# The eight pieces of the shrink in a spectral mixer: two halves, one slot apart, on VectorE alone

## The chip, the cores and the metric

The kernel runs on one NeuronCore of one Trainium2 chip. The metric is the device time of one execution in microseconds (us). A profile of one execution stands beside the times; its span reaches from the first to the last instruction of the program.

## The reference

```python
X = np.fft.rfft(x, axis=1)                  # x: 8 batches x 3072 tokens x 256
Yr = Xr @ w_r - Xi @ w_i + b_r
Yi = Xr @ w_i + Xi @ w_r + b_i
Yr = np.sign(Yr) * np.maximum(np.abs(Yr) - lam, 0.0)      # lam = 0.01
Yi = np.sign(Yi) * np.maximum(np.abs(Yi) - lam, 0.0)
y = np.fft.irfft(Yr + 1j * Yi, n=3072, axis=1)
h = y @ w_in                                # 256 -> 2048
out = (np.maximum(h, 0) + np.log1p(np.exp(-np.abs(h)))) @ w_out     # softplus, 2048 -> 256
```

The step that the change touches is the one with `lam`, the soft threshold. The kernel calls it the shrink: `z - clip(z, -lam, lam)`.

## The kernel before

**The work.** The Fourier transforms are done as products with small matrices in several steps: `s1`, `s3` (forward, with a transposition through memory between them), `mix` (the product with the weights, the bias, the shrink), `s4` (inverse, first half), and `s5` (inverse, second half, which gives tokens). The two layers of the network behind them take most of TensorE's time. All products that need it are done with three matmuls on values split in a high and a low part (`mm3`): the high part is a rounded copy that ScalarE makes, the low part is the rest, which VectorE makes by a subtraction (`low`, L719, and `less`, L119).

**The loop.** The network runs over 192 keys (batch, pair of token blocks, pair of hidden blocks), and each key over four slots, 0 to 3. A slot is written out by hand: first the products of the first layer (`slot_products`), then one step of the transform of a later batch if there is one in this slot (`steps`: one of `s1_four`, `s3`, `mix`, `s4_pair`, `s5`), then small preparations (`fill`: loads, and `fold`, two VectorE operations on the next input), then what earlier slots have put off (`later`), and at last the products of the second layer (`slot_second`). Instructions go to each engine in just this order, and each engine takes them in order.

**The two banks.** The first layer of a key is done with the products of Strassen's kind, seven instead of eight. They are collected in two banks of PSUM, `psc` and `pse`. The three adds of a key that involve `pse` are VectorE's (`add`, L703): it reads `pse` in slots 0, 2 and 3. The matmul that next writes `pse` (slots 1, 3 and 0 of the next key) must come after that add has read it. Behind an add follow, for the same values, ScalarE's softplus (L709), its rounding to the high part (L713), and VectorE's low part (L719), which the second layer needs.

**The mix.** Batches 1 to 7 have 12 mixes each (84), made by `mix_sums`, each one step of one slot. Its 18 to 24 matmuls of 256 columns are followed on VectorE by two adds to `z` (L487, L490), the clipping to `cl` (L491), and the shrink itself: eight pieces (L499) of 32 partitions by 256 columns, since each piece also moves its rows to another place of the tile. The eight pieces are a loop over `e` (the half of the target's partitions), `c` and `g`. In batch 1 the four pieces with `e` = 1 were given to GpSimd, beside VectorE's four. Batch 0 has another mix and isn't touched. The tile `shrunk` is read by `s4_pair`, which takes two mixes at once and stands three (batch 1) or four slots behind the second of them.

The pieces before:

```python
        for e in range(2):
            for c in range(2):
                for g in range(2):
                    src = slice(g * 64 + e * 32, g * 64 + e * 32 + 32), slice(c * D, c * D + D)
                    dst = slice(e * 64 + c * 32, e * 64 + c * 32 + 32), slice(g * D, g * D + D)
                    (nc.gpsimd if b == 1 and e and POOL1 else v).tensor_tensor(out=t[dst], in0=z[src], in1=cl[src], op=ALU.subtract)
```

Of the kernel before, what the change touches and what calls it, by code (L numbers as in the profile page):

```python
# [14 lines left out]
ALU = mybir.AluOpType  # L15
# [13 lines left out]
A22, A11, A12, S1, S2, S3, S4 = range(7)  # L29
B11, B21, T2, T3, T1, B22, T4 = range(7)  # L30
LAM = 0.01
POOL1 = True


@with_exitstack
def tile_spectral_mixer_mlp(ctx, tc, x, w_r, w_i, bias, bias_0, w_in, w_out, f, f_hi, f_lo, g1, g3, g3_hi, g3_lo, hm, out):
# [12 lines left out]
    nc = tc.nc  # L49
# [42 lines left out]
    later = deque()  # L92

    stored = Counter()
# [4 lines left out]
    def store(dst, src, what):  # L99

        queue = nc.scalar if early and what[0] == "d" and stored[what] >= 8 else nc.sync

        def start():
            queue.dma_start(dst, src)
            stored[what] += 1

        later.append(start)
# [140 lines left out]
    def mm3(ps, wh, wl, xh, xl, start, stop, more=False):  # L248
        nc.tensor.matmul(ps, wh, xh, start=start, stop=False, skip_group_check=more)  # L249
        nc.tensor.matmul(ps, wh, xl, start=False, stop=False, skip_group_check=more)  # L250
        nc.tensor.matmul(ps, wl, xh, start=False, stop=stop, skip_group_check=more)  # L251


    def psf():

        if early:
            early.append(None)
            if len(early) % 3:
                return ps_o.tile([P, 512], F32, tag="o", name="psf")
        return ps_f.tile([P, 512], F32, tag="f", name="psf")  # L260
# [182 lines left out]
    def mix(b, gp):  # L443
        assert stored["l", b, gp] == 2
        (mix_direct if b == 0 else mix_sums)(b, gp, *l_t.pop((b, gp)))
# [24 lines left out]
    def mix_sums(b, gp, lh, ll, real):  # L470

        v = nc.vector
        p1, ps = psf(), psf()

        def product(o, what, c, start, stop):
            for k in range(2):
                h, l = [t[:, k, what] if what < 3 else t[:, k] for t in ((lh, ll) if what < 3 else real)]
                mm3(o, h, l, wmh[:, k, c], wml[:, k, c], start and k == 0, stop and k == 1)

        product(p1[:, :D], 2, 0, True, True)  # L480
        product(ps[:, :D], 1, 1, True, True)
        product(ps[:, D:], 0, 2, True, not real)
        if real:
            product(ps[:, D:], 3, 0, False, True)
        z, cl = [sb.tile([P, 512], F32, tag=t, name=t, bufs=1) for t in ("z", "cl")]
        p3 = p1.rearrange("p (c n) -> p c n", c=2)[:, 0:1, :].to_broadcast([P, 2, D])
        v.tensor_tensor(out=z.rearrange("p (c n) -> p c n", c=2), in0=p3, in1=bias_sb, op=ALU.add)  # L487
        if gp == 0:
            v.tensor_tensor(out=z[0:1, D:], in0=p1[0:1, :D], in1=bias_sb[0:1, 0], op=ALU.add)
        v.tensor_tensor(out=z, in0=ps, in1=z, op=ALU.add)  # L490
        v.tensor_scalar(out=cl, in0=z, scalar1=-LAM, scalar2=LAM, op0=ALU.max, op1=ALU.min)  # L491

        t = sb.tile([P, 512], F32, tag=("sh", "sl")[gp % 2], name="shrunk", bufs=1)
        for e in range(2):
            for c in range(2):
                for g in range(2):
                    src = slice(g * 64 + e * 32, g * 64 + e * 32 + 32), slice(c * D, c * D + D)
                    dst = slice(e * 64 + c * 32, e * 64 + c * 32 + 32), slice(g * D, g * D + D)
                    (nc.gpsimd if b == 1 and e and POOL1 else v).tensor_tensor(out=t[dst], in0=z[src], in1=cl[src], op=ALU.subtract)  # L499
        s_t[b, gp] = t  # L500

    def s4(b, gp):
# [18 lines left out]
    def s4_pair(b, pp):  # L521

        if pp == 0:
            d_dr[b] = dram.tile([N1, N2, D], F32, tag="d", name="d_dr")
        banks = psf(), psf()
        both = [s_t.pop((b, 2 * pp + j)) for j in range(2)]
        for j in range(2):
            for kind, c in ((1, slice(0, 512)),) if pp or j else ((0, slice(0, D)), (1, slice(D, 512))):
                for e in range(2):
                    rows, cols = slice(64 * e, 64 * e + 64), slice(64 * j, 64 * j + 64)  # L530
                    nc.tensor.matmul(banks[e][cols, c], g3_half[rows, kind], both[j][rows, c], start=True, stop=True)
        for e, ps in enumerate(banks):
            d = sb.tile([P, 512], F32, tag="d", name="d")
            nc.scalar.copy(d, ps)
            row = 16 * pp + 8 * e
            store(d_dr[b][row:row + 8].rearrange("(g q) n c -> (q n) g c", g=2), d.rearrange("p (g c) -> p g c", g=2), ("d", b))
# [259 lines left out]
    with tc.manual_schedule():  # L796
# [23 lines left out]
        def plan_mix(b, start, step):  # L820
            mixed = done = start
            for gp in range(NP):
                t = product(max(start + step * gp, mixed), s3, b, gp)
                at(max(t - 4, 11), load_a, b, gp)
                mixed = done = product(max(t + (3 if gp else 4), done + 1), mix, b, gp)
                if gp % 2:
                    done = product(mixed + (3 if b == 1 else 4), s4_pair, b, gp // 2)
# [78 lines left out]
        for i in range(min([*fill, *steps]), nt * B + 3):  # L906
            due = len(later)
            if i >= 0:
                g, s = divmod(i, 4)
# [116 lines left out]
```

## Time and profile before

| | |
|---|---|
| median of 3 runs | 2708.27 us (2707.92 to 2711.35) |
| profiled execution, its own time | 2708.41 us |
| its span | 2706.3 us |
| TensorE (PE) busy | 2600.9 us, 96% |
| VectorE (DVE) busy | 1756.7 us, 65% |
| ScalarE (ACT) busy | 1634.7 us, 60% |
| GpSimd (POOL) busy | 201.3 us, 7% |

A row of the timeline says when an instruction began (us from the span's start), how long it took, its engine, line and operation, the tile it writes and those it reads, and in brackets how long its engine had stood idle before it and what it waited for. Matmuls overlap, so their starts tell more than their durations: two matmuls of 512 columns in a row start 0.23 us apart. Names of tiles are the program's: `pse` and `psc` are the two banks, `pso` the banks of the second layer, `psf` those of the transform.

### The profile page before, as it was taken

To read this page: it belongs to the slowest core of one execution; us is meant where nothing else is said; L and a number is where in the kernel's file an instruction comes from. 1 tells how busy PE (TensorE), PEld (TensorE's weight loads), DVE (VectorE), ACT (ScalarE), POOL (GpSimd) and SP (SyncE) were. 2 spreads that over 40 slices of the span, in tenths; PEclk is the share of its full clock that TensorE was granted. 3 is DMA by queue.
4 is the path that set the end of the run, shared out by engine and by line. 5 is a ranking of instruction groups with operands and counts; after the bars stand their busy time and mean duration, and the time that the engine had idled before them with its cause. 6 is when DMAs were issued, how large, how long until landed. Compare 5 with 4: busy or idle time off the path is not lost.

```text
span 2706.3 us, 36636 instructions
## 1 busy us (share of the span) xinstructions
PE 2600.9 (96%) x13252; PEld 2089.2 (77%) x13252; DVE 1756.7 (65%) x3016; ACT 1634.7 (60%) x2940; POOL 201.3 (7%) x245
## 2 busy tenths in 40 slices
PE   8899999999999999999999999999999999999999
PEld 5677778777787777877778777787777787788887
DVE  4888766676566765667756677566774666644554
ACT  4666556556665556665566556665566555666665
POOL 2322210000000000000000000000000000000000
PEclk9999999999999999999999999999999999999999
DMA  7875555655655555464565555556545455455543
GB/s 230 257 227 185 173 166 176 189 170 162 189 166 174 168 166 188 161 190 152 171 194 172 166 175 157 188 171 178 180 152 178 156 160 180 138 159 176 179 153 111
DMA packets 186944, 472.37 MB, mean 175 GB/s; under 512 B 22236, under 2 KB 88700, under 8 KB 186764
## 3 DMA queue, kind: packets, MB, share of 16 engines
q1 hardware_dynamic: 182780, 466.07, 55.0%
q0 software_dynamic: 2624, 2.32, 0.4%
q8 instruction: 105, 1.72, 0.3%
q10 hardware_dynamic: 1360, 1.64, 0.2%
q14 instruction: 75, 0.61, 0.1%
HBM read 382.89 MB, written 82.71 MB: 172 GB/s over the span
## 4 chain that ended last, share of the span: by engine, by line
PE 74%; DVE 19%; issue 2%; DMA 2%; ACT 2%; POOL 1%; SPq 0%; DVEq 0%; ACTq 0%; POOLq 0%
PE pso L249 10%; PE pso L251 10%; PE pso L250 10%; DVE shrunk L499 8%; PE psc L249 5%; PE psc L251 5%; PE pse L249 5%; PE psc L250 5%; PE pse L251 4%; PE pse L250 4%; PE psf L570 4%; PE psf L251 2%; PE psf L249 2%; PE psf L250 2%; DVE t L703 2%
## 5 line engine op out<-in xcount | busy, mean ns | idle before, releaser
L719 DVE TENSOR_TENSOR gl<-t,gh 128x512 fp32r<-128x512 f32 x768 | 537.6, 700 | 322.0 <-ACT gh L713 319.8
L698 ACT COPY t<-psc 128x512 f32<-128x512 f32 x576 | 337.6, 586 | 541.5 <-PE psc L251 540.6
L703 DVE TENSOR_TENSOR t<-pse,t 128x512 f32<-128x512 f32 x576 | 396.1, 688 | 404.5 <-ACT t L698 289.5
L249 PE MATMUL pso<-gh,w 128*128 128x512 f32 x1536 | 627.6, 409 | 0.0
L251 PE MATMUL pso<-gh,w 128*128 128x512 f32 x1536 | 601.4, 392 | 0.0
L250 PE MATMUL pso<-gl,w 128*128 128x512 f32 x1536 | 601.0, 391 | 0.0
L713 ACT CAST gh<-t 128x512 fp32r<-128x512 f32 x768 | 476.9, 621 | 61.9 <-PE pso L251 37.9
L709 ACT ACTIVATE t<-t 128x512 f32<-128x512 f32 x576 | 365.2, 634 | 149.5 <-DVE t L703 149.5
L249 PEld LDWEIGHTS pso<-gh,w 128*128 128x128 f32 x1536 | 290.3, 189 | 121.4 <-issue 72.7
L251 PEld LDWEIGHTS pso<-gh,w 128*128 128x128 f32 x1536 | 289.3, 188 | 63.6
L250 PEld LDWEIGHTS pso<-gl,w 128*128 128x128 f32 x1536 | 290.4, 189 | 48.7
L249 PE MATMUL psc<-y_sb,w 128*128 128x512 f32 x768 | 301.9, 393 | 7.3 <-ACT t L709 3.6
L249 PE MATMUL pse<-y_sb,w 128*128 128x512 f32 x576 | 235.1, 408 | 74.1 <-DVE t L703 73.4
L251 PE MATMUL psc<-y_sb,w 128*128 128x512 f32 x768 | 299.9, 391 | 0.0
L250 PE MATMUL psc<-y_sb,w 128*128 128x512 f32 x768 | 299.2, 390 | 0.0
L499 DVE TENSOR_TENSOR shrunk<-z,cl 32x256 f32<-32x256 f32 x624 | 275.9, 442 | 10.1
L609 POOL TENSOR_TENSOR y_sb<-raw,y_sb 128x512 fp32r<-128x512 f32 x69 | 99.1, 1437 | 2083.8 <-ACT y_sb L606 2083.6
L250 PE MATMUL pse<-y_sb,w 128*128 128x512 f32 x576 | 225.1, 391 | 0.2 <-DVE y_sb L625 0.2
L251 PE MATMUL pse<-y_sb,w 128*128 128x512 f32 x576 | 225.1, 391 | 0.0
L249 PEld LDWEIGHTS pse<-y_sb,w 128*128 128x128 f32 x576 | 108.1, 188 | 131.8 <-DVE t L703 110.3
L249 PEld LDWEIGHTS psc<-y_sb,w 128*128 128x128 f32 x768 | 144.5, 188 | 41.9 <-ACT t L709 6.2
L251 PEld LDWEIGHTS psc<-y_sb,w 128*128 128x128 f32 x768 | 144.4, 188 | 31.6
(167 smaller groups left out, 3225.5 us busy)
## 6 DMA issues: line engine op xcount, KB each, us to landing
w<-w_dr SPq DMA_DIRECT2D x190, 896.0 KB
w<-w_dr SPq DMA_DIRECT2D x185, 512.0 KB
out_y<-ot SPq DMA_DIRECT2D x96, 256.0 KB
dp<-d_dr SPq DMA_DIRECT2D x57, 384.0 KB
ap<-a_dr SPq DMA_DIRECT2D x168, 128.0 KB
d_dr<-d SPq DMA_DIRECT2D x84, 256.0 KB
x<-in_x SPq DMA_DIRECT2D x104, 192.0 KB
a_dr<-a SPq DMA_DIRECT2D x102, 192.0 KB
```

What stands on the lines that cost most here:

```text
L249: nc.tensor.matmul(ps, wh, xh, start=start, stop=False, skip_group_check=more)
L250: nc.tensor.matmul(ps, wh, xl, start=False, stop=False, skip_group_check=more)
L251: nc.tensor.matmul(ps, wl, xh, start=False, stop=stop, skip_group_check=more)
L499: (nc.gpsimd if b == 1 and e and POOL1 else v).tensor_tensor(out=t[dst], in0=z[src], in1=cl[src], op=ALU.subtract)
L570: nc.tensor.matmul(ps[:, t - blk * BLK:t - blk * BLK + n], d_sb[b, blk // 2, n2 // 4][0][:, n2 % 4, k * P:(k + 1) * P], d_sb[b, blk // 2, ...
L609: eng.tensor_tensor(out=lo, in0=raw[j], in1=hi.bitcast(F32), op=ALU.subtract)
L698: nc.scalar.copy(t, banks[bank])
L703: nc.vector.tensor_tensor(out=t, in0=banks[bank], in1=t, op=ALU.add)
L709: nc.scalar.activation(t, banks[bank] if bank else t, AF.Softplus)
L713: nc.scalar.copy(gh, ct[key, what])
L719: nc.vector.tensor_tensor(out=gl, in0=ct.pop((key, what)), in1=gh.bitcast(F32), op=ALU.subtract)
```

## The change

The four pieces with `e` = 0 stay where they were. The four with `e` = 1 are put on the list `later`, so they are issued in the next slot, behind that slot's own products, step and preparations. All are VectorE's now, in batch 1 too. A counter asserts that both halves have been issued before `s4_pair` reads the tile.

```diff
-POOL1 = True
@@ mix_sums
         t = sb.tile([P, 512], F32, tag=("sh", "sl")[gp % 2], name="shrunk", bufs=1)
-        for e in range(2):
+
+        def lay(e):
             for c in range(2):
                 for g in range(2):
                     src = slice(g * 64 + e * 32, g * 64 + e * 32 + 32), slice(c * D, c * D + D)
                     dst = slice(e * 64 + c * 32, e * 64 + c * 32 + 32), slice(g * D, g * D + D)
-                    (nc.gpsimd if b == 1 and e and POOL1 else v).tensor_tensor(out=t[dst], in0=z[src], in1=cl[src], op=ALU.subtract)
+                    v.tensor_tensor(out=t[dst], in0=z[src], in1=cl[src], op=ALU.subtract)
+            stored["s", b, gp] += 1
+
+        lay(0)
+        later.append(lambda: lay(1))
         s_t[b, gp] = t
@@ s4_pair
         both = [s_t.pop((b, 2 * pp + j)) for j in range(2)]
+        assert stored["s", b, 2 * pp + 1] == 2
```

VectorE's order behind a mix in slot 2 with no step in the next slot (batch 3, eighth mix), before. `gl` is a low part, `t<-pse` the add that reads the bank, numbers tell tiles apart:

```order
L491 TENSOR_SCALAR cl_8650<-z_8649 128x512
L499 TENSOR_TENSOR shrunk_8654<-z_8649,cl_8650 32x256 x8
L719 TENSOR_TENSOR gl_8684<-t_8626,gh_8678 128x512
L703 TENSOR_TENSOR t_8613<-pse_8606,t_8613 128x512
L719 TENSOR_TENSOR gl_8708<-t_8680,gh_8682 128x512
L703 TENSOR_TENSOR t_8703<-pse_8699,t_8703 128x512
```

The same place in the changed program, whose lines from the pieces on are five lower:

```order
L490 TENSOR_SCALAR cl_8650<-z_8649 128x512
L499 TENSOR_TENSOR shrunk_8654<-z_8649,cl_8650 32x256 x4
L724 TENSOR_TENSOR gl_8680<-t_8626,gh_8674 128x512
L708 TENSOR_TENSOR t_8613<-pse_8606,t_8613 128x512
L499 TENSOR_TENSOR shrunk_8654<-z_8649,cl_8650 32x256 x4
L724 TENSOR_TENSOR gl_8708<-t_8676,gh_8678 128x512
L708 TENSOR_TENSOR t_8703<-pse_8699,t_8703 128x512
```

The second half has moved behind the first low part and add, and stands ahead of the second ones.

VectorE's order behind a mix in slot 2 with an `s3` in the next slot (batch 3, seventh mix), before. `l<-psf` and `sum` are the two operations of `s3` on VectorE, `ot` is a store's copy:

```order
L499 TENSOR_TENSOR shrunk_8507<-z_8502,cl_8503 32x256 x8
L740 COPY ot_8528<-pso_7443 128x512
L719 TENSOR_TENSOR gl_8543<-t_8479,gh_8537 128x512
L703 TENSOR_TENSOR t_8450<-pse_8443,t_8450 128x512
L119 TENSOR_TENSOR l_8551<-psf_8546,l_8551 128x2x256
L421 TENSOR_TENSOR sum_8552<-psf_8546,sum_8552 128x256
L719 TENSOR_TENSOR gl_8582<-t_8539,gh_8541 128x512
L703 TENSOR_TENSOR t_8577<-pse_8573,t_8577 128x512
```

And in the changed program:

```order
L499 TENSOR_TENSOR shrunk_8507<-z_8502,cl_8503 32x256 x4
L745 COPY ot_8524<-pso_7443 128x512
L724 TENSOR_TENSOR gl_8539<-t_8479,gh_8533 128x512
L708 TENSOR_TENSOR t_8450<-pse_8443,t_8450 128x512
L118 TENSOR_TENSOR l_8547<-psf_8542,l_8547 128x2x256
L420 TENSOR_TENSOR sum_8548<-psf_8542,sum_8548 128x256
L499 TENSOR_TENSOR shrunk_8507<-z_8502,cl_8503 32x256 x4
L724 TENSOR_TENSOR gl_8582<-t_8535,gh_8537 128x512
L708 TENSOR_TENSOR t_8577<-pse_8573,t_8577 128x512
```

The second half has moved behind the add of the next slot and behind both operations of `s3`.

VectorE's order behind a mix in slot 1 with an `s3` in the next slot (batch 3, fifth mix), before:

```order
L499 TENSOR_TENSOR shrunk_8185<-z_8180,cl_8181 32x256 x8
L703 TENSOR_TENSOR t_8207<-pse_8149,t_8207 128x512
L119 TENSOR_TENSOR l_8215<-psf_8210,l_8215 128x2x256
L421 TENSOR_TENSOR sum_8216<-psf_8210,sum_8216 128x256
L719 TENSOR_TENSOR gl_8244<-t_8207,gh_8238 128x512
L703 TENSOR_TENSOR t_8156<-pse_8149,t_8156 128x512
```

And in the changed program:

```order
L499 TENSOR_TENSOR shrunk_8185<-z_8180,cl_8181 32x256 x4
L708 TENSOR_TENSOR t_8203<-pse_8149,t_8203 128x512
L118 TENSOR_TENSOR l_8211<-psf_8206,l_8211 128x2x256
L420 TENSOR_TENSOR sum_8212<-psf_8206,sum_8212 128x256
L499 TENSOR_TENSOR shrunk_8185<-z_8180,cl_8181 32x256 x4
L724 TENSOR_TENSOR gl_8244<-t_8203,gh_8238 128x512
L708 TENSOR_TENSOR t_8156<-pse_8149,t_8156 128x512
```

Here too the second half has moved behind the first add and the operations of `s3`, and stands ahead of the second add. The orders of TensorE and ScalarE are the same in both programs; GpSimd loses 48 pieces.

## Rows read from the trace of the kernel before

**Rows 1.** Page, part 1: busy us (share of the span) xinstructions.

```profile
PE 2600.9 (96%) x13252; PEld 2089.2 (77%) x13252; DVE 1756.7 (65%) x3016; ACT 1634.7 (60%) x2940; POOL 201.3 (7%) x245
```

**Rows 2.** Waits of TensorE, whole span: us in total, times, longest us.

```profile
PE pse L249 <- DVE t L703: 73.4, 73, 2.6
...
PE psc L249 <- ACT t L709: 3.6, 6, 0.6
```

**Rows 3.** Waits of TensorE in the mixes of batch 1, then of batch 3.

```profile
PE pse L249 <- DVE t L703: 5.4, 8, 1.4
...
PE pse L249 <- DVE t L703: 11.1, 10, 2.6
```

**Rows 4.** Groups of instructions by form, VectorE: xcount | busy us, mean ns | idle.

```profile
L499 DVE TENSOR_TENSOR shrunk<-z,cl 32x256 f32<-32x256 f32 x624 | 275.9, 442 | 10.1
```

**Rows 5.** Timeline behind the eighth mix of batch 3, ScalarE, VectorE and TensorE.

```profile
935.21 0.62 ACT L713 CAST gh<-t 128x512 fp32r<-128x512 f32 x1
...
936.54 3.42 DVE L499 TENSOR_TENSOR shrunk<-z,cl 32x256 f32<-32x256 f32 x8
...
939.72 0.39 PE L251 MATMUL psc<-y_sb,w 128*128 128x512 f32 x1
...
940.00 0.69 DVE L719 TENSOR_TENSOR gl<-t,gh 128x512 fp32r<-128x512 f32 x1
...
940.61 0.68 DVE L703 TENSOR_TENSOR t<-pse,t 128x512 f32<-128x512 f32 x1
...
941.35 0.50 PE L249 MATMUL pse<-y_sb,w 128*128 128x512 f32 x1 [1.24 <-DVE t L703]
...
941.68 0.39 PE L250 MATMUL pse<-y_sb,w 128*128 128x512 f32 x1
...
942.15 1.06 PE L365 MATMUL psf<-ap 128*128 128x128 f32 x8
...
944.41 0.39 PE L249 MATMUL psc<-y_sb,w 128*128 128x512 f32 x1
```

**Rows 6.** Timeline of TensorE behind the mix of batch 3 with a fold.

```profile
834.97 0.50 PE L249 MATMUL pse<-y_sb,w 128*128 128x512 f32 x1 [2.57 <-DVE t L703]
...
835.77 1.50 PE L365 MATMUL psf<-ap 128*128 128x128 f32 x8
...
839.62 0.41 PE L249 MATMUL psc<-y_sb,w 128*128 128x512 f32 x1
```

**Rows 7.** Stretch behind it: length, TensorE busy (x), granted clock, DMA share, GB/s.

```profile
836.90:839.60 2.70, 2.70 (x8) 0.50 1.04 233
```

**Rows 8.** Timeline behind the seventh mix of batch 3, VectorE and TensorE.

```profile
928.82 0.68 DVE L703 TENSOR_TENSOR t<-pse,t 128x512 f32<-128x512 f32 x1
...
930.28 0.39 PE L249 MATMUL pse<-y_sb,w 128*128 128x512 f32 x1
```

**Rows 9.** Timeline behind the fifth mix of batch 3, VectorE, ScalarE and TensorE.

```profile
888.06 3.43 DVE L499 TENSOR_TENSOR shrunk<-z,cl 32x256 f32<-32x256 f32 x8
...
889.91 0.59 ACT L380 CAST l<-psf 128x512 fp32r<-128x512 f32 x1
...
892.27 0.50 PE L249 MATMUL pse<-y_sb,w 128*128 128x512 f32 x1 [0.61 <-DVE t L703]
...
894.17 0.68 DVE L703 TENSOR_TENSOR t<-pse,t 128x512 f32<-128x512 f32 x1
...
895.13 0.40 PE L249 MATMUL pse<-y_sb,w 128*128 128x512 f32 x1
```

**Rows 10.** Timeline behind the tenth mix of batch 3, ScalarE and TensorE.

```profile
978.99 0.59 ACT L592 CAST y_sb<-psf 128x512 fp32r<-128x512 f32 x1 [0.70 <-PE psf L570]
...
983.98 0.50 PE L249 MATMUL psc<-y_sb,w 128*128 128x512 f32 x1 [0.60 <-ACT t L709]
```

**Rows 11.** Timeline behind the fourth mix of batch 1, VectorE.

```profile
251.92 3.04 DVE L499 TENSOR_TENSOR shrunk<-z,cl 32x256 f32<-32x256 f32 x4
...
254.99 1.12 DVE L719 TENSOR_TENSOR gl<-t,gh 128x512 fp32r<-128x512 f32 x1
```

## The prediction, made before the changed kernel ran

> **What bounds the kernel now.** I read the page's first part, then the waits of TensorE, then those waits in single batches, then the timeline around one wait of each kind. TensorE is busy 96% of the span [rows 1], so only time that it stands still can be won. The table of waits names one large cause: the first matmul into the bank pse waits for VectorE's add at L703, 73.4 us in 73 waits [rows 2]; everything else after the start is small (ScalarE's softplus into psc: 3.6 us in 6). One middle batch holds 11.1 us of it in 10 waits, batch 1 holds 5.4 in 8 [rows 3]. The waits stand behind the mixes of batches 1 to 7: pse is read by an add; that add stands on VectorE behind the shrink's eight pieces of the mix one slot earlier; and TensorE may not write pse before the add has read it. VectorE's pieces are 275.9 us in all [rows 4], and VectorE as a whole is far from full (65%, [rows 1]): its order hurts, not its load.
>
> **What one wait costs.** Take the eighth mix of batch 3 [rows 5]. The pieces run from 936.54 for 3.42 us (0.43 each), then the low part at L719 (940.00), then the add (940.61). TensorE's matmul into pse starts at 941.35, 0.74 after the add's start. The matmul before it was issued at 939.72 and matmuls follow each other by 0.23, so pse was due at 939.95: 1.40 lost. The next one comes 0.33 behind instead of 0.23, another 0.10. So a wait that reads 1.24 in its row costs 1.50.
>
> **The change, part by part.** No arithmetic goes away. 4 of 8 pieces (4 x 0.43 = 1.72 us) leave their slot and stand at the end of the next slot's VectorE work; in batch 1, 12 x 4 pieces come over from GpSimd. TensorE, ScalarE and the queues keep their order, and the pair product that reads the shrunk tile comes at least two slots after the second half, so nobody waits for that half itself. What counts is which add stands behind which half. There are five kinds of mix.
>
> (a) *Mix in slot 2 or 3 of a key, no s3 in the next slot:* 25 of 84 (four each in batches 2 to 6, five in batch 7), all with the wait of rows 5. After: the first half ends at 936.54 + 1.72 = 938.26. The low part can go at once (its input was written by 935.83, [rows 5]), the add 0.61 later at 938.9, TensorE at 939.64, before 939.95. No wait is left, with 0.3 to spare. The second half then runs to 941.3, and the next low part and add follow at 941.3 and 941.9, which frees the bank at 942.7; the next matmul into pse then comes about 943.6 (without the s3 step in that stretch, 942.6). So the second half fits, in the tightest case by nothing. 25 x 1.50 = **37.5 us**.
>
> (b) *The same with a fold behind the pieces:* 5 mixes (batches 2 to 6). [...] From the s3 product to the second psc behind it takes 839.62 - 835.77 = 3.85 [rows 6], where the same work in rows 5 takes 944.41 - 942.15 = 2.26: the clock costs 1.6. After: the add is 1.72 sooner, the wait reads about 0.85. Waits up to 1.24 leave the clock at full speed (the matmuls behind 941.35 in rows 5 are 0.23 apart soon after), so I take the clock's part as won too: 5 x (1.72 + 1.59) = **16.5 us**.
>
> (c) *Slot 2, with s3 behind it:* 12 mixes in batches 2 to 7. The first add is free, as in (a). But the second half stands ahead of the second add, so both halves are ahead of it as before: it stays at 928.82, the bank is free at 929.56, and the matmul that now comes at 930.28 [rows 8] can come no sooner. 0.72 is won, 0.10 lost again on the restart: 0.62. For the other half of these, whose s3 waits for ScalarE's copy, it is less. I take 0.45, ends 0 and 0.62: **5.4 us**.
>
> (d) *Slot 1, with s3 behind it:* 12 mixes. Here the chain runs through both adds. First half from 888.06 to 889.78, add 889.80, then the s3 copy's low part, which waits for ScalarE until 890.50 [rows 9], 890.54, the sum 891.14, second half 891.58 to 893.30, low part, add at 893.93. That add is now at 894.17 [rows 9]; TensorE goes at 894.67 instead of 895.13. 0.46 less 0.10: 0.35 here, where the first wait alone would promise 0.87. I take 0.25, ends 0 and 0.35: **3.0 us**.
>
> (e) *The rest.* Six mixes with a token product (s5) behind them: the add starts a chain over ScalarE (softplus, rounding, softplus of the next) at whose end psc waits 0.60 [rows 10], 0.76 + 0.10 by the reckoning above. ScalarE's copy of the tokens ends at 979.58 [rows 10] and sets the chain then, about 1.3 sooner than now, which is enough: 6 x 0.85 = **5.1 us**. The first two mixes of each batch have both halves ahead of the next add that matters: 0. Batch 1: four pieces on VectorE beside four on GpSimd take 3.04 instead of 1.72, and the low part beside the first of them 1.12 instead of 0.69 [rows 5, 11]. The first add comes 1.3 to 1.7 sooner, which ends the waits (5.4 us in the rows, about 7 by issue), but the second half that GpSimd did is now ahead of the second add, some 0.4 later than now. I take **4 us**, ends 0 and 7.
>
> Cutting the shrink in two is not free on VectorE. In rows 5 the add starts 0.08 before the low part ahead of it has ended; behind the pieces the next instruction starts 0.03 after their end. Each cut thus adds about 0.1 at either side, and the walks above hold it (starts behind a half are taken without overlap). [...]
>
> **Sum.** 37.5 + 16.5 + 5.4 + 3.0 + 5.1 + 4 = 71.5 us. The profiled execution took 2708.4 us (its span 2706.3), the median of three is 2708.27, so one stands for the other: 2708.4 - 71.5 = **2637 us**, 2.6% less.
>
> **Rivals.**
> *The wait moves to ScalarE.* Behind each add stand softplus, rounding, low part; row 983.98 [rows 10] shows TensorE waiting for that chain already. For: ScalarE is 60% busy. Against: in rows 5 its input was there 0.7 before the pieces began. If each mix of kinds (a), (b) and (d) (42) met 0.76 of it, 32 us would go: 2669.
> *The second half is hidden better than the walks say* (the second add of (c) and (d) has slack, batch 1 gives all): of some 29 us that these kinds and the first mixes now lose, the sum takes 12; with all of it 2620, less the rest of (b) 2615.
> *The second half takes the wait's place everywhere.* Place: the low part and add of the slot after next, where kind (a) had 0.0 to 0.9 of room. Price: 1.72 + 0.10 at each mix; it outweighs the 71.5 from 39 of 84 mixes on; at 60 it is 109, so 2746, slower. Against: rows 5 give the room, and only (c) and (d), 24 mixes, lack it, which the sum holds.
> *It does nothing*, because pse waits for something that only looks like the add: 2708. Against: TensorE starts 0.74 after the add's start in rows 5, whatever ends before.
>
> **How the numbers follow.** Forecast 0.74, ScalarE 0.09, better hidden 0.09, second half everywhere 0.05, nothing 0.03. The forecast's own bounds: down to 2624 if (c), (d) and batch 1 give their upper ends and the tightest of (a) too, up to 2661 if the clock's part of (b) stays lost (8) and (c), (d) and batch 1 give nothing (12), with 4 for (e). To leave out no more than 2 in 10 the range reaches a little into both neighbours: 2618 to 2664. What a measurement of this kernel can tell from no change is about 0.2% (5.4 us). Faster by more than that: 0.92; within: 0.03; slower: 0.05.
>
> **What would show it.** In the waits of the changed kernel, pse behind L708 (the same add, five lines lower) should fall from 73 us to some 15 to 25, mostly short waits of 0.3 to 0.6 in kinds (c) and (d) and one of about 1.0 per batch behind its first mix. In kind (a) none should be left. The clock should be 1.00 behind the fold of (b). Pieces: 672 on VectorE, 0.43 each in every batch, none on GpSimd. Wrong would be: new waits of psc for ScalarE at most mixes, waits of pse in kind (a), or GpSimd's other work falling on the second halves (pieces of 0.8 us and more outside batch 1).

## The result and the profile after

The changed kernel takes **2640.01 us** (median of 4 runs, 2639.20 to 2640.61); the kernel before, timed beside it on the same chip, 2708.1. The ratio is 0.9748 [0.9731, 0.9765] (in brackets, here and below, the 95% interval): 2.5% less, 68 us. Forecast were 2637 us with a range of 2618 to 2664. The profiled execution took 2639.2 us, its span 2637.4, which is 68.9 below the span before.

The first part of the page (busy us, share of the span, instructions) and the shares of the chain that ended last, changed kernel:

```profile
PE 2581.6 (98%) x13252; PEld 2086.4 (79%) x13252; DVE 1762.0 (67%) x3064; ACT 1631.7 (62%) x2940; POOL 159.9 (6%) x197
...
PE 83%; DVE 11%; DMA 2%; ACT 2%; issue 2%; SPq 0%; POOL 0%; ACTq 0%; DVEq 0%; POOLq 0%
```

Against [rows 1], VectorE has 48 instructions and 5.3 us more, the 48 pieces that came from GpSimd. TensorE does the same 13252 matmuls and has 19 us less busy time: part of what it was busy with before was matmuls at the lower clock (two of 512 columns start 0.43 us apart in the stretch of [rows 7], at 0.50, where they otherwise start 0.23 apart). So not only time that TensorE stood still could be won, as the prediction's first paragraph has it. In the chain VectorE's share fell from 19% to 11%.

Waits of TensorE over the whole span, changed kernel (us in total, times, longest), and below them its group of pieces (xcount | busy us, mean ns | idle):

```profile
PE pse L248 <- DVE t L708: 28.7, 48, 1.6
...
PE psc L248 <- ACT t L703: 1.6, 3, 0.8
...
L499 DVE TENSOR_TENSOR shrunk<-z,cl 32x256 f32<-32x256 f32 x672 | 279.9, 417 | 12.2
```

The waits for the add fell from 73.4 us in 73 to 28.7 in 48, and the longest from 2.6 to 1.6 [rows 2]. That is 45 us for a gain of 68. The rest is what a wait costs beyond its own row: the 0.1 at each restart (0.33 instead of 0.23 behind the first matmul in [rows 5]), gaps of about 0.1 that stand in no list (in the trace before, pse at 981.03 comes 0.33 behind psc), and the clock. No wait for ScalarE took its place (1.6 in 3; in [rows 2] softplus into psc cost 3.6 in 6). The mean piece fell from 442 to 417 ns, since batch 1's, 3.04 us for four beside GpSimd's [rows 11], now take 1.69 to 1.72 [rows 4].

The kind that carries the sum, (a), at the place of [rows 5]: behind the eighth mix of batch 3, VectorE and TensorE, changed kernel.

```profile
914.75 1.70 DVE L499 TENSOR_TENSOR shrunk<-z,cl 32x256 f32<-32x256 f32 x4
916.47 0.69 DVE L724 TENSOR_TENSOR gl<-t,gh 128x512 fp32r<-128x512 f32 x1
917.08 0.68 DVE L708 TENSOR_TENSOR t<-pse,t 128x512 f32<-128x512 f32 x1
917.80 1.72 DVE L499 TENSOR_TENSOR shrunk<-z,cl 32x256 f32<-32x256 f32 x4
919.54 0.69 DVE L724 TENSOR_TENSOR gl<-t,gh 128x512 fp32r<-128x512 f32 x1
920.15 0.68 DVE L708 TENSOR_TENSOR t<-pse,t 128x512 f32<-128x512 f32 x1
...
917.92 0.39 PE L250 MATMUL psc<-y_sb,w 128*128 128x512 f32 x1
918.14 0.39 PE L248 MATMUL pse<-y_sb,w 128*128 128x512 f32 x1
```

The add stands behind four pieces; TensorE goes from psc to pse 0.22 later, without a bracket, so without a wait. The second half lies between the two adds, and the second one is early enough too. This is the walk of the prediction, step by step.

### The profile page after: what moved, and what is told of

Same layout as the page of the kernel before. It is cut to its first block, busy times and chain, and to the rows that moved or that the text cites. A ratio compares the mean times of both kernels' runs of the same rounds, so it can differ in the third digit from the quotient of the medians.

```text
span 2637.4 us, 36619 instructions
## 1 busy us (share of the span) xinstructions
PE 2581.6 (98%) x13252; PEld 2086.4 (79%) x13252; DVE 1762.0 (67%) x3064; ACT 1631.7 (62%) x2940; POOL 159.9 (6%) x197
## 3 DMA queue, kind: packets, MB, share of 16 engines
q8 instruction: 105, 1.72, 0.3%
## 4 chain that ended last, share of the span: by engine, by line
PE 83%; DVE 11%; DMA 2%; ACT 2%; issue 2%; SPq 0%; POOL 0%; ACTq 0%; DVEq 0%; POOLq 0%
PE pso L248 12%; PE pso L250 11%; PE pso L249 11%; PE psc L248 6%; PE psc L250 6%; PE psc L249 6%; PE pse L248 5%; PE pse L249 4%; PE pse L250 4%; PE psf L575 4%; DVE shrunk L499 3%; PE psf L364 2%; PE psf L250 2%; PE psf L249 2%; PE psf L248 2%; PE psf L329 2%
## 5 line engine op out<-in xcount | busy, mean ns | idle before, releaser
L248 PE MATMUL pse<-y_sb,w 128*128 128x512 f32 x576 | 230.8, 401 | 29.8 <-DVE t L708 28.7
L248 PEld LDWEIGHTS psc<-y_sb,w 128*128 128x128 f32 x768 | 144.3, 188 | 33.4 <-ACT t L703 3.1
L250 PEld LDWEIGHTS psc<-y_sb,w 128*128 128x128 f32 x768 | 144.2, 188 | 31.4
L249 PEld LDWEIGHTS psc<-y_sb,w 128*128 128x128 f32 x768 | 144.3, 188 | 30.4
```

## Where the 69 us came from, kind by kind

Each mix has one clipping (L491 before, L490 after). The time from one mix's clipping to the next, before less after, says what that mix's surroundings won. Summed over the two profiled executions:

| kind | mixes | forecast us | won us | each |
|---|---|---|---|---|
| (a) slot 2 or 3, no s3 next | 25 | 37.5 | 38.2 | 1.47 to 1.58 |
| (b) with a fold | 5 | 16.5 | 13.4 | 3.3 in three, 1.71 in two |
| (c) slot 2, s3 next | 12 | 5.4 | 3.35 | 0.45 and 0.23, one -0.13 |
| (d) slot 1, s3 next | 12 | 3.0 | 2.6 | 0.35 and 0.12 to 0.15 |
| (e) s5 behind | 6 | 5.1 | 7.5 | 1.23 to 1.25 |
| first two of a batch | 12 | 0 | -1.5 | down to -0.29 |
| batch 1 | 12 | 4 | 3.85 | |
| sum | 84 | 71.5 | 67.4 | |

The remaining 1.5 us lie ahead of the first mix, in the first 190 us. The ten kernels of this document have the same instructions there, and in their traces that stretch takes 187.9 to 195.0 us without following the edits, so the 1.5 us say nothing of the change.

## Experiments

Three theories stood against each other. **W** is the prediction's: the time is the waits of pse for the add, each by the pieces that stand ahead of it on VectorE, plus what a restart costs; GpSimd's share plays no part outside batch 1. **G**: the gain comes from taking GpSimd out. **D**: the gain comes from delay alone, so that the whole block, put off uncut, would do as well or better. **K**, beside W, is the clock's share of a long wait. Edits are shown against the changed kernel, where nothing else is said.

### GpSimd's part by itself: unsplit_vector and split_pool

All eight pieces on VectorE in one block, which is the kernel before with one line changed:

```diff
-POOL1 = True
+POOL1 = False
```

> The move to VectorE alone: eight pieces in one go in every batch. Theory W: in batch 1 eight pieces take 3.43 us instead of 3.04 for four beside GpSimd's, and the low part behind them 0.69 instead of 1.12, so the adds stand where they stood: 2708 us (2705 to 2712), waits of pse within 1 us of the 73 of before. Theory G: part of the 68 us is here, 2700 us or less.

Measured: 2708.39 us (2706.58 to 2713.79), ratio to before 1.0006 [0.9996, 1.0015]. Waits of TensorE, whole span and then batches 2 to 7 (440 to 2400 us):

```profile
PE pse L249 <- DVE t L703: 76.3, 76, 2.6
...
PE pse L249 <- DVE t L703: 65.5, 61, 2.6
```

The second row is the one of the kernel before in that stretch (65.6 in 61). The first is 2.9 above the 73.4 of before, where the expectation allowed 1: the difference lies in batch 1, which took 3.0 us longer in this trace from its first clipping to the first of batch 2. The times can't tell 3 us from nothing here. So taking GpSimd out, alone, wins nothing.

The halves with batch 1's second one on GpSimd:

```diff
-                    v.tensor_tensor(out=t[dst], in0=z[src], in1=cl[src], op=ALU.subtract)
+                    (nc.gpsimd if b == 1 and e else v).tensor_tensor(out=t[dst], in0=z[src], in1=cl[src], op=ALU.subtract)
```

> The split alone: two halves one slot apart, but in batch 1 the second half stays on GpSimd, as it was before the change. Theory W (what counts is what stands on VectorE ahead of the next add that reads pse): batches 2 to 7 win as in the changed kernel, about 64 us; in batch 1 the adds have only four pieces ahead of them, so it wins 6 to 7 us instead of the 4 of the changed kernel: 2637 us (2633 to 2641). Theory G (the gain comes from taking GpSimd's pieces away): 2700 us or more.

Measured: 2642.74 us (2642.21 to 2644.68), ratio to before 0.9765 [0.9751, 0.978]. G, which had 2700 or more, falls: 65 us are there without touching GpSimd. But W had expected 2637, and from the first to the last mix of batch 1 this kernel took 5.9 us more than the changed one. Behind the fourth mix of batch 1, VectorE and GpSimd:

```profile
265.33 3.04 DVE L499 TENSOR_TENSOR shrunk<-z,cl 32x256 f32<-32x256 f32 x4
268.40 1.12 DVE L724 TENSOR_TENSOR gl<-t,gh 128x512 fp32r<-128x512 f32 x1
...
265.44 3.54 POOL L499 TENSOR_TENSOR shrunk<-z,cl 32x256 f32<-32x256 f32 x4 [11.69 <-DVE cl L490]
```

The instructions of the second half stand a slot later in the program, and still they start 0.11 after VectorE's first ones. GpSimd's queue holds nothing else there (idle 11.69 us); it waits for the clipping alone and goes. Putting them off put them behind no other work, so VectorE's four still take 3.04 and the low part 1.12, just as in [rows 11]. The same place in the changed kernel, VectorE:

```profile
249.53 1.70 DVE L499 TENSOR_TENSOR shrunk<-z,cl 32x256 f32<-32x256 f32 x4
251.26 0.69 DVE L724 TENSOR_TENSOR gl<-t,gh 128x512 fp32r<-128x512 f32 x1
...
253.93 1.71 DVE L499 TENSOR_TENSOR shrunk<-z,cl 32x256 f32<-32x256 f32 x4
```

Against the kernel before, batch 1 took 2.1 us longer, all of it at its first mix; the other eleven agree with before within 0.03 each. There the granted clock was low for 6.8 us in this trace and for 3.4 in the one before, so that loss need not be the halves' doing. So in batch 1 the two parts of the change need each other: halves alone win nothing, VectorE alone wins nothing, both win 3.85.

### Later without a cut: whole_later

```diff
-        lay(0)
-        later.append(lambda: lay(1))
+        later.append(lambda: (lay(0), lay(1)))
```

> All eight pieces one slot later, undivided. Theory W, walked through kind by kind as in the prediction: kind (a) keeps its 37.5 us, (b) wins 1.1 more each; but in kind (d) the pieces no longer fill VectorE's wait for ScalarE's copy and 1.7 us more stand ahead of the second add (12 mixes, 20 us lost against the changed kernel), the same at the first mix of each batch (10 us) and behind s5 (8 us), and about 5 in batch 1: 2682 us (2670 to 2692), waits of pse about 65 us. Theory D (the later, the better): 2630 us or less.

Measured: 2736.7 us (2735.09 to 2744.46), ratio to before 1.0119 [1.0102, 1.0135]. It is slower than the kernel before, and 97 us slower than the halves. D falls, and W's size was wrong by 55. Waits of TensorE over the whole span, and the core's span and mean granted clock:

```profile
PE pse L248 <- DVE t L707: 88.4, 52, 3.2
...
core 0: 2734.1 us, clock 0.984
```

Fewer waits than before (52 against 73), but long ones. By kind, against the halves: (a) keeps its gain whole (-0.1 at most, but -1.0 at the very last mix), (b) wins 4.0, but (d) loses 28.5, (c) 26.3, the first two mixes of the batches 18.5, (e) 10.4, batch 1 19. The fifth mix of batch 3, kind (d), VectorE and TensorE:

```profile
900.95 0.69 DVE L118 TENSOR_TENSOR l<-psf,l 128x512 fp32r<-128x512 f32 x1 [0.48 <-ACT l L379]
...
901.89 3.42 DVE L499 TENSOR_TENSOR shrunk<-z,cl 32x256 f32<-32x256 f32 x8
905.34 0.69 DVE L723 TENSOR_TENSOR gl<-t,gh 128x512 fp32r<-128x512 f32 x1
905.95 0.68 DVE L707 TENSOR_TENSOR t<-pse,t 128x512 f32<-128x512 f32 x1
906.69 0.50 PE L248 MATMUL pse<-y_sb,w 128*128 128x512 f32 x1 [1.89 <-DVE t L707]
```

And the stretch behind that wait (length, busy of TensorE, its loads, VectorE, ScalarE, GpSimd, granted clock, DMA share, GB/s):

```profile
907.60:910.90 3.30, 3.30 (x12) 1.44 (x12) 2.58 (x4) 1.60 (x4) 0.00 (x0) 0.50 0.09 35
```

All eight pieces now stand between the s3 step and the second add, where VectorE has first stood idle for ScalarE's copy (0.48 in the first row). TensorE stands still for 1.89, and then runs at a granted clock of 0.50 for some 3.3 us. From the first mix on, this trace has the low clock in 20 places, for 82 us in all. The expectation had left it out, and had put (c) at nothing lost. An estimate from the walks by kind: at the price that the clock has behind the fold (1.6 us a place, and four of the 20 are twice as long) it is some 38 us, and (c) without its share of that some 17. These two terms make up the 55 us. This run also prices the rival that ends slower, "the second half takes the wait's place": with twice as many pieces moved it does come true, in the kinds for which the walks had found no room.

### Half the price: half_quarter

The second half is one copy of the tile's lower 64 partitions instead of four pieces (0.43 us instead of 1.72); the lower half of the tile then holds `z`, which the kernel leaves unshrunk:

```diff
-        later.append(lambda: lay(1))
+        def rest():
+            v.tensor_copy(t[64:], z[64:])
+            stored["s", b, gp] += 1
+        later.append(rest)
```

> The second half is one copy of 64 x 512 instead of four subtractions (the lower half of the tile then holds z, not the shrunk values): about 0.45 us instead of 1.72, in the same place as in the changed kernel. Theory W: the price of the second half falls by 1.3 us where it stands ahead of an add: waits of pse fall from 28.7 to about 9 us, 2614 us (2607 to 2622). Theory S: 2635 to 2640, the same waits by another name. Theory H (the second half is hidden already, what is left has other causes): 2640, waits unchanged.

Measured: 2608.98 us (2604.56 to 2613.39), ratio 0.9645 [0.9629, 0.9661]. Waits over the whole span:

```profile
PE pse L248 <- DVE t L713: 8.0, 13, 1.5
```

With 1.3 us less of VectorE work per mix, and nothing else moved, 31 us go. So what the changed kernel still waits for is the second half's own time ahead of the second add, as the walks of (c), (d) and the first mixes say.

### Out of the second add's way: two_slots and two_slots_late

If that is so, the second half only has to stand one slot further back.

```diff
-        later.append(lambda: lay(1))
+        later.append(lambda: later.append(lambda: lay(1)))
```

> The second half two slots behind the first instead of one. Theory W: it then stands behind the second add in the mixes of slot 1 and 2 with s3 behind them, and behind the add that the first mix of each batch waits for; the waits of pse that the changed kernel has left (28.7 us in 48) fall to 8 to 12, mostly one of 1.0 per batch behind the fold: 2612 us (2604 to 2622). Theory S (ScalarE's chain behind the add takes over): 2632 to 2640, with waits of psc for ScalarE instead.

Measured: 2622.31 us (2617.65 to 2624.51), ratio 0.9686 [0.9671, 0.9701]; W had 2612 with 2604 to 2622, so a narrow miss. Waits of TensorE in batch 1 (185 to 400 us), and in batches 2 to 7 (440 to 2400):

```profile
PE psf L536 <- DVE shrunk L499: 1.8, 2, 1.6
...
PE pse L248 <- DVE t L708: 4.9, 6, 0.8
```

In batches 2 to 7 the changed kernel has 21.8 us in 36 in that stretch; 4.9 in 6 are left, and 25.6 us were won: 8.9 at the first mixes, 3.5 at the fifth, 3.5 at the sixth, 6.0 at the seventh, 3.5 at the eleventh. W had 28. Batch 1 lost 7.7, and its rows show two places. `s4_pair` stands only three slots behind there, and now waits for the half itself (1.57 behind the fourth mix, a new wait; 2.1 us lost). And at the first mix, where 3.1 us are lost, one second half now falls ahead of an add. TensorE, two waits there, and the clock behind the first (length, busy, granted clock, DMA share, GB/s):

```profile
207.59 0.51 PE L248 MATMUL pse<-y_sb,w 128*128 128x512 f32 x1 [1.73 <-DVE t L708]
...
210.54 1.98 PE L329 MATMUL psf<-x,f 48*64 48x512 f32 x6 [0.97 <-DVE raw L607]
...
210.00:214.00 4.00, 3.46 (x10) 0.50 0.00 2
```

In the changed kernel the same pse wait reads 0.77, and the clock stays at 1.00. That the longer wait lowered the clock is still not shown: two_slots_fold, the last run below, has the changed kernel's order in batch 1 and its two waits, and there the clock fell all the same.

```profile
207.47 0.50 PE L248 MATMUL pse<-y_sb,w 128*128 128x512 f32 x1 [0.79 <-DVE t L708]
...
210.41 1.98 PE L329 MATMUL psf<-x,f 48*64 48x512 f32 x6 [0.98 <-DVE raw L607]
...
210.00:217.00 7.00, 6.59 (x17) 0.52 0.26 87
```

It cost that trace 2.9 us at the first mix against two_slots_late, whose waits there are the same and whose clock stayed at 1.00. So most of the 3.1 us is probably the clock, which can fall there without the longer wait. The repair is to leave batch 1 at one slot:

```diff
-        later.append(lambda: lay(1))
+        later.append((lambda: lay(1)) if b == 1 else (lambda: later.append(lambda: lay(1))))
```

> Two slots between the halves in batches 2 to 7, one slot in batch 1. Theory W: batches 2 to 7 as in the run with two slots (25.6 us less than the changed kernel between their first and last mix), batch 1 as in the changed kernel: 2614 us (2609 to 2620), waits of pse about 12 us. If the loss of the run with two slots in its first part was chance and not batch 1's later second half, 2622.

Measured: 2614.57 us (2610.89 to 2617.8), ratio 0.9661 [0.9647, 0.9676], as expected; batch 1 is the changed kernel's within 0.02 us. Waits in 440 to 2400 us are again 4.9 in 6.

### The fold's price: fold_moved and two_slots_fold

Term (b) came out lower than forecast. Is its place worth what the prediction says when only the fold moves? In the kernel before, the pieces stay, and the fold behind the third mix of batches 2 to 6 goes one slot later:

```diff
-                at(t - 2 if b == 1 else t - 4, fold, b, c)
+                at(t - 2 if b == 1 else t - 3 if t - 4 in (106, 202, 298, 394, 490) else t - 4, fold, b, c)
```

> The kernel before, with the fold behind the third mix of batches 2 to 6 put one slot later, so that it no longer stands ahead of the add. Theory W: the wait of 2.57 becomes one of 1.24 there (5 x 1.33 = 6.7 us). Theory K (the granted clock of 0.50 behind that wait in batches 2, 3 and 5 is a consequence of the long wait): it stays at full speed there, 3 x 1.6 = 4.8 us more: 2696 us (2693 to 2700). If the clock falls for another reason, 2701 us (2699 to 2704), with the low clock still in these three places.

Measured: 2694.3 us (2693.88 to 2696.99), ratio to before 0.9958 [0.9944, 0.9973], within the expectation; at the five places 11.45 us were won, 5 x 1.33 for the fold and 3 x 1.6 for the clock. The stretches behind that mix in batches 2 to 6, kernel before (length, TensorE busy, granted clock, DMA share, GB/s):

```profile
501.80:505.00 3.20, 3.20 (x13) 0.50 1.00 276
836.30:839.50 3.20, 3.20 (x11) 0.50 1.03 223
1171.00:1174.20 3.20, 3.20 (x16) 1.00 1.03 249
1502.00:1505.10 3.10, 3.10 (x12) 0.50 1.00 239
1836.90:1840.10 3.20, 3.20 (x16) 1.00 1.04 253
```

The same wait stands in all five; the clock fell in three. unsplit_vector has the same instructions in these batches, and there it fell in batches 2, 4 and 6. Its stretches behind the mix of batches 3 and 4:

```profile
836.00:839.00 3.00, 3.00 (x16) 1.00 1.05 268
...
1167.70:1170.70 3.00, 3.00 (x11) 0.50 1.02 234
```

So it is not the batch that decides. From one clipping to the next the same mix took 1.61 to 1.65 us longer with the low clock than without (batches 3 to 6, these two traces): that is its price, with nothing else changed. With the fold moved, the three places (batches 2, 3 and 5), and the waits of the whole span:

```profile
496.00:510.00 14.00, 12.96 (x72) 1.00 0.98 252
827.00:840.00 13.00, 12.04 (x66) 1.00 0.97 264
1488.00:1502.00 14.00, 12.76 (x70) 1.00 0.98 236
...
PE pse L249 <- DVE t L703: 67.2, 73, 1.6
```

The clock stays at 1.00, in all five batches, where with the long wait it fell at six of ten places of the two traces; the longest wait is 1.6. Both together, two slots in batches 2 to 7 and the fold a slot later:

> The same with the fold behind the third mix of batches 2 to 6 one slot later. Theory W: the wait of 1.0 that is left there goes, 5 x 1.1 us: 2609 us (2604 to 2615), waits of pse about 7 us, none longer than 0.9 behind batch 1.

Measured: 2608.76 us (2606.75 to 2613.13), ratio to before 0.9638 [0.9622, 0.9654], as expected; 7.9 us in 13 waits of pse are left, one of them (0.7) in batches 2 to 7. This beats both kernels: 3.6% below the one before, 31 us below the changed one.

## Why the prediction was right, point by point

**What bounds the kernel: right.** The waits of pse for an add that stands behind the pieces were the whole matter. Moving GpSimd's part alone gave 0 (unsplit_vector), the halves without it 65 us (split_pool), a cheaper second half 31 more (half_quarter).

**(a): right, 38.2 for 37.5.** What the prediction added to the row's 1.24 (the matmul that was due at once, and the restart) was right: the places won 1.47 to 1.58, not 1.24. By the rows alone it would have been 31.

**(b): right in mechanism, too large by 3.1.** The step that failed is "5 x (1.72 + 1.59)": it took the clock of [rows 7] (0.50, behind the wait of 2.57 in [rows 6]), one place in batch 3, for all five. The clock fell in three (rows above), and which three changes from one trace to the next. Behind the changed kernel's mix, TensorE:

```profile
817.25 0.50 PE L248 MATMUL pse<-y_sb,w 128*128 128x512 f32 x1 [0.84 <-DVE t L708]
...
820.00:823.00 3.00, 3.00 (x15) 2.47 (x14) 2.82 (x6) 2.04 (x4) 0.00 (x0) 1.00 1.02 256
```

The wait reads 0.84 where "about 0.85" was forecast, and the last row (the 1.00 behind the five engines' busy times is the clock) shows the clock at full speed behind it, as it is in all five batches of this trace. That no wait up to 1.24 lowers it, as the prediction has it, doesn't hold in general: in two_slots_fold, above, it fell behind stops of 0.79 and 0.98. The same stretch in all five batches gives 5 x 1.72 + 3 x 1.59 = 13.4, which is what was won.

**(c): right in mechanism, 3.35 for 5.4, within its ends.** The second half does stand ahead of the second add. The seventh mix of batch 3, changed kernel:

```profile
905.26 1.72 DVE L499 TENSOR_TENSOR shrunk<-z,cl 32x256 f32<-32x256 f32 x4
907.61 0.68 DVE L708 TENSOR_TENSOR t<-pse,t 128x512 f32<-128x512 f32 x1
908.35 0.50 PE L248 MATMUL pse<-y_sb,w 128*128 128x512 f32 x1 [0.61 <-DVE t L708]
```

The wait of 0.61 is new: it has moved to the second bank write, where [rows 8] shows none. **(d): right, 2.6 for 3.0.** At the fifth mix the wait fell from 0.61 [rows 9] to 0.31, the restart stays:

```profile
870.72 1.72 DVE L499 TENSOR_TENSOR shrunk<-z,cl 32x256 f32<-32x256 f32 x4
873.07 0.68 DVE L708 TENSOR_TENSOR t<-pse,t 128x512 f32<-128x512 f32 x1
873.81 0.50 PE L248 MATMUL pse<-y_sb,w 128*128 128x512 f32 x1 [0.31 <-DVE t L708]
```

**(e): too small, 7.5 for 5.1.** At the tenth mix psc now comes without a wait, 0.23 behind the matmul before it, as forecast, since the tokens' copy set the chain: VectorE's operation on the tokens waits 0.37 for it. The price was only that row's 0.60 and its restart; the 1.24 won per place hold the small gaps of pse of about 0.1, and their restarts, that the same stretch also had and that the sum left out.

**First mixes: 0 forecast, 1.5 us lost.** Both halves are ahead of the add there as before, so the cut itself shows: at the first mix of batch 3 the add began 6.05 us after the clipping before, 6.30 after. Behind the second half, changed kernel:

```profile
783.71 0.69 DVE L745 COPY ot<-pso 128x512 f32<-128x512 f32 x1
784.43 0.69 DVE L708 TENSOR_TENSOR t<-pse,t 128x512 f32<-128x512 f32 x1
```

The add starts 0.03 after the copy's end; before, with no piece ahead of the copy, it started 0.08 ahead of that end. The prediction had put 0.1 at each side of a cut, but charged it in the walks alone and not here. No run shows what sets the two starts.

**Batch 1: 3.85 for 4**, though the walk behind it held GpSimd's and VectorE's parts for separate gains, which they are not (split_pool).

**The waits left: 28.7 us, where 15 to 25 were named.** By kind they are 8.0 behind the first mixes (1.26 a batch, not about 1.0), 6.0 in (c), 4.2 in (b), 3.7 in (d) and none in (a), which is the picture that was named. It left out 4.5 in batch 1 and 2.4 ahead of the first mix.

**The rivals.** The wait did not move to ScalarE (1.6 us in 3). "Better hidden" is what two_slots_late made of it, with another edit: 25 us more were there to win, but not by this change. "Everywhere slower" came true only in whole_later; by its own price it would outweigh the 71.5 us from 40 mixes on, not 39. The forecast's lower bound isn't fully worked out: the named ends of (c), (d) and batch 1 give 2631, and no row gives the rest of the way to 2624.

**How near it came.** The forecast missed the time by 3 us in 68. By kinds it was 4.1 too large, made of (b) -3.1, (c) -2.1, first mixes -1.5 and (e) +2.4 in the main. That (e) made up for part of the rest is luck.

## What to carry to other kernels

When two engines meet at a bank, write out which instructions stand ahead of each read of it, once before and once after a move. Work that is cut and put off is free only at the places where the next read also has room; here 30 of 84 places held 52 of 67 us, and the same move without the cut was slower than leaving it (+1.2%). Putting work off delays it only where something then stands ahead of it: GpSimd's pieces behind the fourth mix of batch 1, put off by a slot on a queue that was otherwise idle, started 0.11 us after VectorE's first ones, as they had before (split_pool). And a price read at one place (the clock behind the fold) is to be looked at in every place that it is multiplied by, and in a second trace.

## What the runs showed of the hardware that was not expected

- **The clock behind the same stop.** Behind pse waits of about 2.57 us [rows 6] the granted clock fell to 0.50 in three places of five, with the same instructions around them, and in unsplit_vector in three of the same five, not the same three. It fell behind one of 1.89 in whole_later. Behind stops of 0.79 and 0.98 near the start of batch 1 it fell in two_slots_fold and stayed at 1.00 in the changed kernel and in two_slots_late. It stayed at 1.00 behind the waits of 1.24 of kind (a) [rows 5], 25 in the trace before and as many in unsplit_vector. So neither the place nor the length of the one stop decides alone; what does stays open, and no run took it apart.
- **Two engines at the same tile.** VectorE's four pieces took 3.04 us beside GpSimd's four (3.54) and 1.70 alone. The low part that followed took 1.12 instead of 0.69, so GpSimd's pieces also cost instructions that don't touch their tiles.
- **A cut cost 0.25 us on VectorE** at the first mix of batch 3, where everything stands back to back, with no arithmetic added. At the first mixes of batches 2 to 7 the kernel lost 0.15 to 0.29 us.
